# Windowed attention with an MLP mixer: where the loads, the casts and the global columns stand in the instruction order

## The chip, the cores and the metric

The kernel runs on one core of a Trainium2 chip. A core has five engines that each execute their own instructions in order and meet only at semaphores: TensorE (PE, with its weight loads listed as PEld), VectorE (DVE), ScalarE (ACT), GpSimd (POOL) and SyncE (SP). SP computes nothing here: it issues transfers and DMA transposes. POOL issues transfers too. All transfers are carried out by 16 DMA engines. SBUF is the working memory of 128 partitions, PSUM the memory that TensorE writes.

The metric is the device time of one execution in microseconds (us), less is better. A kernel's time is the median of its runs. One execution of each kernel was also taken with the profiler; times inside it count from the start of its span.

## The reference

A batch goes through attention with a window of 32 positions to each side and 8 global positions, and then through an MLP mixer over tokens and channels. Shapes: 8 batches, 8 heads, 576 positions, 64 values for each head; the mixer works on 576 x 512.

```python
def _attn_ref(q, k, v, global_idx):
    scores = scale * np.matmul(q, k.transpose(0, 1, 3, 2))
    mask = np.abs(pos[:, None] - pos[None, :]) <= window
    mask = mask | is_global[:, None] | is_global[None, :]
    scores = np.where(mask, scores, -1000000000.0)
    ...
    return np.matmul(attn, v)

def _moe_ref(x, w_tok1, w_tok2, w_ch1, w_ch2):
    xt = x.transpose(0, 2, 1)
    h = np.maximum(xt @ w_tok1, 0.0) @ w_tok2
    u = x + h.transpose(0, 2, 1)
    h2 = np.maximum(u @ w_ch1, 0.0) @ w_ch2
    return u + h2
```

## The kernel before

**Data.** Heads are taken in four pairs, positions in five tiles, the last of 64. Each batch needs q and k with positions along the free axis. They are loaded as f32 into `lq`, `lk` (1024 KB each) and `lr` (the last 64 positions, twice 128 KB), cast to f16 into `qk` and `rn`, turned, and put in order into `qT` and `kT`. `lq`, `lk`, `lr`, `qk` and `rn` exist once: a load waits until the casts of the batch before have read its buffer, a cast until the turns of the batch before have read its own. `qT` and `kT` exist twice. `qT` also holds eight global columns for each tile, copied by `globals_` (L377) from `gT`, which `gather_t` (L305) makes from the gathered rows of four batches: t=0 for batches 1 to 3, t=1 for batches 4 to 7.

**Two ways to turn.** Batches 0 to 2 are turned on TensorE: `T` (L401) transposes into PSUM, `TE` (L409) copies out of it on DVE with a shuffle, two copies for q and two for k. Batches 3 to 7 are turned by DMA transposes from SP (`turns`, L674), into `raw` and `rawr`, and put in order by DVE copies (`order`, L367).

**Attention of a batch n.** `S_all` (L468) multiplies q and k of one pair into two PSUM tiles of a pool of three (`psS`), and ACT takes their exps in three parts into `e_all`. `SM` (L471) multiplies by the band's mask on DVE. `GK` (L481) makes the rows of the global positions, `gk`, for which all four pairs of `qT` must be ready. `OG` and `PV` make the output x.

**Mixer.** `M1` and `M2` mix tokens and give `u`; `M3` (L607) transposes `u` by DMA from SP into `uT`, two tiles at a time and, after odd batches, the last rows `ul` of two batches. `M4` (L619) gives `b1` with a relu on ACT, `M5` (L644) multiplies by the second weight in two parts for each tile. The second part ends with a DVE add into `osb` and a store from SP. `osb` comes from a pool of three buffers (`ob`, L53), which a store gives back when it has landed. `M4` and `M5` use a PSUM pool of two (`psM`). After an odd batch there are five tiles t0 to t4, the last with the rest of two batches (add at L658, two stores at L660), otherwise four.

**Order.** The order of all instructions is written out by hand and each engine gets its own in that order. `period(b)` (L684) runs the attention of batch n = b + 1 and fills in the channel mixer of batch b: the list `dense` holds its M4 and M5 pieces, and `d(k)` puts in the next k of them. At a period's end some pieces are left over, which the next period begins with. m = b + 2 is the batch whose q and k are prepared meanwhile. In a period the emission is: scores of pairs 0, 1 and 2; GK; from the period of batch 3 on, the turns of m and the load of m + 1; scores of pair 3; OG; five PV with M1 between; M2 and M3; left-over pieces; and, last, `globals_(m)`.

**Loads and casts before.** The load of batch 1 is issued during batch 0; load(2) and load(3) stand at the heads of the periods of batches 1 and 2, load(4) behind the turns of batch 3, load(5) to load(7) behind the turns of 4 to 6. All loads are issued from SP. Batch 2 is cast in one block on ACT at the end of the period of batch 1, batch 3 on POOL during the period of batch 2. Batches 4 to 7 have nine casts each on ACT: three at a period's end, three behind the scores of pair 0 of the next period, three behind those of pair 1. The first of the nine is for `rn`, then q and k of one pair after the other.

Of the kernel before, what the change touches and what calls it, by code (L numbers as in the profile page):

```python
# [18 lines left out]
WIN = 32  # L19
# [7 lines left out]
def kernel(  # L27
# [12 lines left out]
    nc = tc.nc  # L40
    B, H, S, D = q.shape
# [7 lines left out]
    LAST = S - P * (NT - 1)  # L49
# [33 lines left out]
        r1 = P - WIN if c == NT - 1 else P  # L83
        return r0, r1, P * c - WIN + r0

    def load_qk(b, hs):
        for ten, dst in ((q, lq), (k, lk)):
            nc.sync.dma_start(
                out=dst[:, hs].rearrange("p h i d -> p h (i d)"),
                in_=ten[b, hs, 0 : S - LAST, :].rearrange("h (p i) d -> p h (i d)", i=4),  # L90
            )

    def load_rest(b):
        for t, ten in enumerate((q, k)):
            nc.sync.dma_start(
                out=lr[LAST * t : LAST * t + LAST], in_=ten[b, :, S - LAST : S, :].rearrange("h p d -> p h d")
            )

# [238 lines left out]
    def casts(b, eng):  # L337
        return [lambda: cast_qk(b, 0, None, eng)] + [
            lambda ti=ti, p=p: cast_qk(b, ti, p, eng) for p in range(NP) for ti in range(2)
        ]  # L340
# [68 lines left out]
    def TE(b, p):  # L409
        pT = st[b]["pT", p]  # L410
        qT, kT = qTs[b % 2][:, p], kTs[b % 2][:, p]

        pm = pT[:, 0, 0:512].rearrange("p (i t x) -> p t x i", i=4, t=4)
        nc.vector.tensor_copy(out=qT[:, 0:4, GW:QS].rearrange("p t (x i) -> p t x i", i=4), in_=pm)
        nc.vector.tensor_copy(out=qT[:, 4, GW : GW + LAST], in_=pT[:, 1, 512 : 512 + LAST])
        nc.vector.tensor_copy(  # L416
            out=kT[:, WIN : WIN + 512].rearrange("p (x i) -> p x i", i=4),
            in_=pT[:, 1, 0:512].rearrange("p (i x) -> p x i", i=4),
        )
        nc.vector.tensor_copy(out=kT[:, WIN + 512 : WIN + S], in_=pT[:, 1, 512 + LAST : 640])  # L420

    def S_(b, p, part):
        qf = qTs[b % 2][:, p].rearrange("p t x -> p (t x)")
# [44 lines left out]
    def S_all(b, p):  # L468
        return S_(b, p, 0) + S_(b, p, 1)
# [74 lines left out]
    def M1(b, ch):  # L544
        s = st[b]
        if ch == 0 and b == 0:
            s["a1p"] = [psm([P, 512], name=f"a1p_{b}_{tt}") for tt in range(2)]
        elif ch == 0:
            ps = pss([P, 2, 512], name=f"a1p_{b}")
            s["a1p"], s["a1pp"] = [ps[:, 0], ps[:, 1]], ps  # L550
        ps = s["a1p"]
        for tt in range(2):
            w = w1[:, ch, P * tt : P * tt + P] if ch < NT - 1 else w1l[:, b % 2, P * tt : P * tt + P]
            nc.tensor.matmul(ps[tt], lhsT=w, rhs=x16s[b % 2][:, ch, :], start=(ch == 0), stop=(ch == NT - 1))  # L554
        if ch < NT - 1:
            return
        a1 = mb.tile([P, 2, DM], F16, tag="a1", bufs=1, name=f"a1_{b}")
        if b == 0:
            nc.scalar.activation(out=a1[:, 0], in_=ps[0], func=AF.Relu)
            nc.vector.tensor_scalar(out=a1[:, 1], in0=ps[1], scalar1=0.0, scalar2=None, op0=ALU.max)  # L560
        else:
            nc.scalar.activation(out=a1, in_=s["a1pp"], func=AF.Relu)
        s["a1"] = a1
        s["u16"] = mb.tile([P, 4, DM], F16, tag="u16", name=f"u16_{b}")
        if b % 2 == 0:
            s["ul"] = mb.tile([P, DM], F16, tag="ul", name=f"ul_{b}")
        else:
            s["ul"] = st[b - 1]["ul"]
# [95 lines left out]
    def d(k):  # L664
        for _ in range(k):
            if dense:
                dense.pop(0)()

    def load(i):
        if i < B:  # L670
            load_rest(i)
            load_qk(i, slice(0, H))

    def turns(i):  # L674
        turn_rest(i)
        for p in range(NP):
            turn(i, p)

    def cast(i, lo, hi):
        if 3 < i < B:  # L680
            for c in casts(i, nc.scalar.copy)[lo:hi]:
                c()

    def period(b):  # L684
        n, m = b + 1, b + 2
        odd = b % 2
        dense.extend(lambda j=j: M4(b, j) for j in range(NJ))
        if odd:
            dense.extend(lambda j=j: M4l(b, j) for j in range(3))
        dense.extend(lambda t=t, i=i: M5(b, t, i) for t in range(4 + odd) for i in range(2))  # L690
        if n == B:
            d(len(dense))
            return
        tail = len(dense) - (23 if odd else 20) - 2 * odd
        regular = n > 2

        def scores(p):
            es = S_all(n, p)
            es[0]()
            es[1]()  # L700
            d(1)
            es[2]()
            if n < 3 and p < 2:
                T(n, p + 2)
            d(1)
            SM(n, p)
            if n < 3 and p < 2:
                TE(n, p + 2)
            elif n > 2 and p < 2:
                order(n, p + 2)  # L710

        if n == 1:
            load(2)
        elif n == 2:
            load(3)
        scores(0)
        cast(m, 3, 6)
        d(1 if tail > 5 else 0)
        scores(1)
        cast(m, 6, 9)  # L720
        d(max(tail - 4 - (tail > 5), 0))
        scores(2)
        GK(n)
        if regular and m < B:
            turns(m)
            load(m + 1)
        if n == 2:
            for c in casts(3, nc.gpsimd.tensor_copy):
                c()
            turns(3)  # L730
            load(4)
        d(1)
        scores(3)
        d(1)
        OG(n)
        d(1)
        if n == 3:
            gather_t(1)
        fill = [order_rest, lambda i: order_k(i, 0), lambda i: order_q(i, 0), lambda i: order_k(i, 1), lambda i: order_q(i, 1)]
        for tau in range(NT):  # L740
            PV(n, tau)
            if 0 < tau < 4:
                M1(n, tau - 1)
            if regular and m < B:
                fill[tau](m)
            if tau < 4:
                d(1)
        M1(n, 3)
        d(len(dense) - (8 + 2 * odd))
        M1(n, 4)  # L750
        d(1)
        if m < B:
            load_v16(m)
        M2(n, 0)
        M3(n, 0)
        M2(n, 1)
        M3(n, 1)
        M2(n, 2)
        if n % 2:
            M3(n, 2)  # L760
        if n == 1:
            for c in casts(2, nc.scalar.copy):
                c()
            d(2)
            T(2, 0)
            TE(2, 0)
            T(2, 1)
            TE(2, 1)
        else:
            cast(n + 2, 0, 3)  # L770
            d(1)
            if n == 2:
                order_rest(3)
                order(3, 0)
                order(3, 1)
            d(1)
        if m < B:
            globals_(m)

    def cast0(p):  # L780
        cast_qk(0, 0, p, nc.scalar.copy)
# [58 lines left out]
        M1(0, tau - 2)  # L840
    M1(0, NT - 2)
    M1(0, NT - 1)
    M23_first(0)
    M23_first(1)
    M3_first(0)
# [7 lines left out]
    T(1, 1)  # L853
    TE(1, 0)
    TE(1, 1)
    gather_t(0)
    globals_(1)
    qk_pads(1)
    pads(1)
    load_wc2(0)  # L860
# [36 lines left out]
```

## Time and profile before

| | |
|---|---|
| runs | 347.68, 350.14 and 350.29 us |
| median of the runs | 350.14 us |
| profiled execution | 347.81 us, of which its span 346.1 us |
| mean granted clock of TensorE | 0.982 |
| DVE, ACT, POOL busy | 58%, 48%, 21% of the span |
| moved by DMA | 48.18 MB, mean 139 GB/s |

The profiled execution is close to the fastest run. In the profile a line such as `x <- y` names the tile written and the tile read, `L651` the line of the kernel, and the bracket behind a row of the timeline gives how long the engine stood idle before it and what ended that idle time. SPq is SP's queue of issues: the time of such a row is that of the issue, not of the transfer. Times to landing stand in the view of the DMA issues. The granted clock is a share of TensorE's full speed.

### The profile page before, as it was taken

Reading aid. Unit: us, or ns where it says so; the run is one execution under the profiler, and the core shown is the slowest. Engines: PE = TensorE matmul, PEld = TensorE weight load, DVE = VectorE, ACT = ScalarE, POOL = GpSimd, SP = SyncE. Lnnn points to the kernel's source line nnn. Section 1 sums busy time; section 2 is a strip of 40 time slices with the busy share of each in tenths; the row PEclk is TensorE's granted clock in tenths of the full one; section 3 lists DMA queues with packets and bytes.
Section 4 is the critical chain, followed back from the end, with each engine's and each line's share of the span. In section 5 each row is a group of like instructions: output and inputs, shape, how many; then the busy total and the mean of one; then the engine's idle time right before and its main releaser. Section 6 shows DMA issues by size and latency. Waiting matters only on the chain.

```text
span 346.1 us, 6451 instructions
## 1 busy us (share of the span) xinstructions
PE 302.6 (87%) x2541; PEld 157.8 (46%) x2541; DVE 200.6 (58%) x433; ACT 165.3 (48%) x292; POOL 72.3 (21%) x113
## 2 busy tenths in 40 slices
PE   1556859997989979999899999997899999998994
PEld 0334435553436634464346544643356445543641
DVE  5898767648396456675757456763763666351021
ACT  2438137605482346732973577335945247303600
POOL 8879535100069100040004000310000000000000
PEclk9999989999899989999999999999999999999998
DMA  5999999603889992599549964999350421033013
GB/s 156 255 294 155 225 247 196 39 32 91 239 186 127 228 229 76 108 127 296 150 112 134 290 128 102 112 226 238 93 93 17 110 77 30 0 76 123 0 63 91
DMA packets 114526, 48.18 MB, mean 139 GB/s; under 512 B 89408, under 2 KB 109760, under 8 KB 114496
## 3 DMA queue, kind: packets, MB, share of 16 engines
q1 hardware_dynamic: 77008, 39.60, 49.3%
q0 software_dynamic: 37200, 8.16, 29.1%
q8 instruction: 20, 0.33, 0.4%
q14 instruction: 10, 0.08, 0.1%
q10 hardware_dynamic: 288, 0.01, 0.0%
HBM read 36.12 MB, written 9.44 MB: 132 GB/s over the span
## 4 chain that ended last, share of the span: by engine, by line
PE 62%; DVE 16%; DMA 9%; ACT 7%; SPq 3%; issue 2%; ACTq 0%; DVEq 0%
PE op L651 21%; PE b1p L625 18%; DMA lk<-in_k_dram 8%; PE a1p L554 4%; PE s L431 3%; PE b1lp L638 3%; DVE e_all L479 3%; PE hp L578 3%; ACT e_all L444 3%; PE pv L531 2%; PE pv L522 2%; PE pv L527 2%; DVE kT L416 2%; ACT b L628 1%; ACT e_all L457 1%
## 5 line engine op out<-in xcount | busy, mean ns | idle before, releaser
L625 PE MATMUL b1p<-uT,wc 128*128 128x512 f16 x384 | 96.1, 383 | 5.4 <-DVE osb L655 4.3
L651 PE MATMUL op<-wc,b 128*128 128x512 f16 x384 | 90.8, 389 | 0.0
L628 ACT ACTIVATE b<-b1p 128x512 f16<-128x512 f32 x96 | 58.5, 609 | 64.9 <-PE b1p L625 64.6
L651 PEld LDWEIGHTS <-b 128*128 128x128 f16 x384 | 37.2, 99 | 45.8 <-issue 3.4
L625 PEld LDWEIGHTS <-wc 128*128 128x128 f16 x384 | 34.9, 98 | 48.5 <-issue 10.9
L655 DVE TENSOR_TENSOR osb<-u,op 128x512 f32<-128x512 f16 x32 | 21.9, 685 | 53.5 <-PE op L651 50.2
L324 POOL DMA_DIRECT2D vsh<-in_v_dram x35 | 29.9, 865 | 103.9 <-PE pv L531 101.1
L444 ACT ACTIVATE e_all<-s 128x832 f16<-128x832 f32 x32 | 27.8, 869 | 39.4 <-issue 20.6
L479 DVE TENSOR_TENSOR e_all<-e_all,bandm 128x1040 f16<-128x1040 f16 x64 | 43.7, 723 | 1.2
L584 DVE TENSOR_TENSOR u<-x,hp 128x512 f16<-128x512 f16 x28 | 17.4, 682 | 22.1 <-PE hp L578 22.1
L431 PE MATMUL s<-qT,kT 64*128 64x208 f16 (+1 forms) x320 | 20.9, 257 | 10.4 <-DVE qT L378 6.3
L539 DVE TENSOR_TENSOR x<-pv,rr 128x512 f16<-128x512 f32 (+1 forms) x40 | 27.6, 691 | 1.4
L522 PEld LDWEIGHTS <-e_all 128*128 128x128 f16 x320 | 22.1, 100 | 5.5 <-issue 0.5
L473 DVE TENSOR_TENSOR eg<-e_all,bandm 128x160 f16<-128x160 f16 x32 | 7.8, 245 | 28.8 <-ACT e_all L462 28.6
L522 PE MATMUL pv<-vsh,e_all 128*128 128x66 f16 x320 | 24.4, 197 | 0.0
L431 PEld LDWEIGHTS <-kT 64*128 64x128 f16 x320 | 12.5, 98 | 25.2 <-issue 16.1
L335 ACT CAST qk<-lq 128x512 f16<-128x512 f32 x28 | 17.8, 634 | 12.3 <-DMA lq<-in_q_dram 12.2
L457 ACT ACTIVATE e_all<-s 128x576 f16<-128x576 f32 x32 | 21.0, 657 | 3.2 <-PE s L431 3.2
L538 DVE RECIPROCAL rr<-pv 128x8 f32<-128x8 f32 (+1 forms) x40 | 8.3, 207 | 23.1 <-PE pv L531 22.9
L527 PE MATMUL pv<-vsh,e_all 128*128 128x66 f16 x256 | 21.1, 198 | 0.0
L335 ACT CAST qk<-lk 128x512 f16<-128x512 f32 x24 | 15.3, 638 | 11.6 <-DMA lk<-in_k_dram 11.6
L527 PEld LDWEIGHTS <-e_all 128*128 128x128 f16 x256 | 17.9, 101 | 3.5 <-issue 0.2
(154 smaller groups left out, 348.4 us busy)
## 6 DMA issues: line engine op xcount, KB each, us to landing
out_dram<-osb SPq DMA_DIRECT2D x32, 256.0 KB, 2.3
lq<-in_q_dram SPq DMA_DIRECT2D x7, 1024.0 KB, 7.4
lk<-in_k_dram SPq DMA_DIRECT2D x7, 1024.0 KB, 10.3
wc<-in_moe_w_ch_dram POOLq DMA_DIRECT2D x6, 512.0 KB, 12.9
vsh<-in_v_dram POOLq DMA_DIRECT2D x21, 128.0 KB, 5.8
vsh<-in_v_dram POOLq DMA_DIRECT2D x14, 96.0 KB, 6.2
lq<-in_q_dram SPq DMA_DIRECT2D x4, 256.0 KB, 5.3
lk<-in_k_dram SPq DMA_DIRECT2D x4, 256.0 KB, 5.7
```

What stands on the lines that cost most here:

```text
L324: nc.gpsimd.dma_start(out=vsh[b % 2][r0:r1, c, :, 0:D], in_=v[b, :, j0 : j0 + (r1 - r0), :].rearrange("h p d -> p h d"),)
L335: eng(out=qk[:, ti, p].rearrange("q i (r d) -> q r i d", r=2), in_=(lq, lk)[ti][:, hs])
L431: nc.tensor.matmul(ps[:, par, off : off + n], lhsT=kT[r, P * c : P * c + P], rhs=qf[r, lo : lo + n], start=True, stop=True,)
L444: nc.scalar.activation(out=e2[:, :, 1:3, 64:EW], in_=ps[:, :, 0 : 2 * W].rearrange("p h (c x) -> p h c x", c=2), func=AF.Exp, scale=scale,)
L457: nc.scalar.activation(out=o, in_=ps[:, :, 0 : 2 * QS].rearrange("p h (c x) -> p h c x", c=2), func=AF.Exp, scale=scale)
L479: nc.vector.tensor_mul(out=eh, in0=eh, in1=bandm)
L522: nc.tensor.matmul(o, lhsT=e_all[:, h, tau, EW - P - sh : EW - sh], rhs=vsh[b % 2][:, tau, h, :], start=hh == 0, stop=False,)
L527: nc.tensor.matmul(o, lhsT=e_all[:, h, tau + 1, 0:P], rhs=vsh[b % 2][:, tau + 1, h, :], start=False, stop=False)
L539: nc.vector.tensor_tensor(out=x16s[b % 2][r, tau, :].rearrange("p (f h x) -> p f h x", f=2, h=NP), in0=pq[r, :, :, 0:D], in1=rr[r].unsquee ...
L625: nc.tensor.matmul(ps, lhsT=wc1[:, cc, P * j : P * j + P], rhs=s["uT"][:, cc, :], start=(cc == 0), stop=(cc == 3))
L628: nc.scalar.activation(out=s["b1"][:, j, :], in_=ps, func=AF.Relu)
L651: nc.tensor.matmul(ps, lhsT=w, rhs=wc2[:, j, :], start=(j == 0), stop=(j == NJ - 1))
```

## The change

- Loads: at the head of a period of batch n >= 3 the kernel issues load(n + 2), ahead of the scores and of everything that the period issues from SP. Before, that load stood behind the turns of n + 1 in the same period. Load(2) goes out through POOL; load(3) and load(4) stay where they were.
- Casts: the nine casts of a batch from 4 on stand in one block on ACT at the end of the period before, behind M3 and ahead of the left-over pieces.
- Left-over pieces: the pieces that stood behind the scores of pairs 0 and 1 (with the casts) now stand within them, ahead of `SM` and `order`. No product on TensorE changes its place by this.
- Global columns: `globals_(m)` stands ahead of the last but one M1 instead of at the period's end; `gather_t(0)` and `globals_(1)` stand ahead of `M23_first`, instead of behind the shuffles of batch 1.
- The k copies of `TE` for pairs 0 and 1 of batch 1 go from DVE to ACT.

```diff
-    def load_qk(b, hs):
+    def load_qk(b, hs, eng=None):
         for ten, dst in ((q, lq), (k, lk)):
-            nc.sync.dma_start(
+            (eng or nc.sync).dma_start(
...
+        copy_k = nc.scalar.copy if b == 1 and p < 2 else nc.vector.tensor_copy
...
-        nc.vector.tensor_copy(
+        copy_k(
             out=kT[:, WIN : WIN + 512].rearrange("p (x i) -> p x i", i=4),
...
-        nc.vector.tensor_copy(out=kT[:, WIN + 512 : WIN + S], in_=pT[:, 1, 512 + LAST : 640])
+        copy_k(out=kT[:, WIN + 512 : WIN + S], in_=pT[:, 1, 512 + LAST : 640])
...
     def load(i):
+        eng = nc.gpsimd if i == 2 else nc.sync
         if i < B:
-            load_rest(i)
-            load_qk(i, slice(0, H))
+            load_rest(i, eng)
+            load_qk(i, slice(0, H), eng)
...
-        def scores(p):
+        def scores(p, k):
...
-            d(1)
+            d(1 + k)
             SM(n, p)
...
-        if n == 1:
-            load(2)
-        elif n == 2:
-            load(3)
-        scores(0)
-        cast(m, 3, 6)
-        d(1 if tail > 5 else 0)
-        scores(1)
-        cast(m, 6, 9)
-        d(max(tail - 4 - (tail > 5), 0))
-        scores(2)
+        load(2 if n == 1 else 3 if n == 2 else n + 2)
+        scores(0, tail > 5)
+        scores(1, max(tail - 4 - (tail > 5), 0))
+        scores(2, 0)
         GK(n)
         if regular and m < B:
             turns(m)
-            load(m + 1)
...
+        if m < B:
+            globals_(m)
         M1(n, 3)
...
+        later = 2 if n == 1 else n + 2
+        if later < B:
+            for c in casts(later, nc.scalar.copy):
+                c()
         if n == 1:
-            for c in casts(2, nc.scalar.copy):
-                c()
             d(2)
...
         else:
-            cast(n + 2, 0, 3)
             d(1)
...
-        if m < B:
-            globals_(m)
...
     M1(0, NT - 1)
+    gather_t(0)
+    globals_(1)
     M23_first(0)
...
-    gather_t(0)
-    globals_(1)
     qk_pads(1)
```

More of the change, by code (lines that the diff above doesn't have):

```diff
@@ L91, in load_qk, with load_rest @@
             )
-    def load_rest(b):
+    def load_rest(b, eng=None):
         for t, ten in enumerate((q, k)):
-            nc.sync.dma_start(
+            (eng or nc.sync).dma_start(
                 out=lr[LAST * t : LAST * t + LAST], in_=ten[b, :, S - LAST : S, :].rearrange("h p d -> p h d")
@@ L677, in turns @@
             turn(i, p)
-    def cast(i, lo, hi):
-        if 3 < i < B:
-            for c in casts(i, nc.scalar.copy)[lo:hi]:
-                c()
     def period(b):
@@ L732, in period @@
         d(1)
-        scores(3)
+        scores(3, 0)
         d(1)
@@ L760, in period @@
             M3(n, 2)
+        later = 2 if n == 1 else n + 2
+        if later < B:
+            for c in casts(later, nc.scalar.copy):
+                c()
         if n == 1:
-            for c in casts(2, nc.scalar.copy):
-                c()
             d(2)
```

## The prediction

> **What bounds the kernel now.** I read the page's head first, then PE's idle gaps in the timeline, the granted clock around them, and last what fills SP's queue. A head is the start of a period, where the scores of the next batch begin; heads are numbered by that batch, 1 to 7.
>
> ```profile
> span 346.1 us, 6451 instructions
> PE 302.6 (87%) x2541; PEld 157.8 (46%) x2541; DVE 200.6 (58%) x433; ACT 165.3 (48%) x292; POOL 72.3 (21%) x113
> ```
>
> TensorE is busy for 87% of the span and executes in order, so a piece of another engine counts only where it makes PE wait. These places are the heads: the scores need shuffled q and k, global columns, exps on ACT and free buffers at once. The view by windows shows two of them (columns: stretch, its length, PE, PEld, DVE, ACT and POOL busy, granted clock, DMA share, GB/s).
>
> ```profile
> 45.90:50.05 4.15, 0.39 (x4) 0.20 (x4) 3.72 (x14) 0.00 (x0) 1.03 (x1) 1.00 1.34 275
> 50.05:53.50 3.45, 3.45 (x23) 2.03 (x24) 0.00 (x0) 2.00 (x4) 1.72 (x2) 0.51 2.22 174
> 84.40:87.00 2.60, 0.02 (x2) 0.02 (x4) 2.52 (x9) 0.00 (x0) 0.00 (x0) 1.00 0.51 99
> 87.60:91.00 3.40, 3.40 (x16) 1.82 (x15) 0.00 (x0) 1.64 (x3) 0.00 (x0) 0.50 0.74 171
> ```
>
> PE does nothing for 3.8 and 2.6 us while DVE is busy, and then runs some 3.4 us at half clock. Such a gap costs its length and 1.7 us (half of 3.4) behind it.
>
> **First head: gathered rows and two copies.** The rows are DVE, DVE, then PE.
>
> ```profile
> 45.17 0.68 DVE L587 TENSOR_TENSOR ul<-x,hp 64x512 f16<-64x512 f16 x1 [1.10 <-PE hp L578]
> ...
> 48.56 0.20 DVE L308 CAST g_q<-g_q 128x128 f16<-128x128 f32 x1
> ```
> ```profile
> 50.05 0.94 PE L431 MATMUL s<-qT,kT 64*128 64x208 f16 x10 [0.87 <-DVE qT L378]
> ```
> ```profile
> 85.34 0.68 DVE L414 COPY qT<-pT 128x512 f16<-128x512 f16 x1
> ...
> 86.73 0.19 DVE L378 COPY qT<-gT 128x160 f16<-128x160 f16 x1
> ```
>
> Today `ul` (45.17) is followed by both pairs' shuffles, then by gathered rows and global columns from 48.56, and the scores start at 50.05, 1.49 us later. The change puts that block ahead of M23_first, where PE and DVE wait for each other anyway. There it costs between nothing and its 1.49 us; I take 0.8, the middle. After `ul` (0.68) only the first pair's q copies are left, one copy of 0.68 (row at 85.34) and a short one: the next group of four copies starts 1.39 us (86.73 - 85.34) after this pair's begin, so q is half, 0.7. The k copies go to ACT beside it. Scores start at about 45.2 + 0.8 + 0.7 + 0.7 = 47.4, 2.65 us sooner, and the half clock (1.7) should go, since PE's gap shrinks below 1 us. That is 4.35; I take 4.1, because the next shuffles still follow the exps on DVE.
>
> Load(2) moves to POOL. It is issued behind gather(1) and its data is first read by the casts at the end of the period (before the gap at 84.40), so I cost it at nothing. POOL has room for four issues:
>
> ```profile
> POOL rn L332 <- PE pT L406: 32.3, 1, 32.3
> ```
>
> Were the cover gone, the casts and with them head 2 would be late by the overhang.
>
> **Second head: global columns earlier.** Scores wait for the global columns (86.73, 0.19) behind the second pair's shuffles; afterwards only for the first pair, done at 85.34. The gap loses 1.6 us (86.92 - 85.34), is then 1.0, and the half clock behind it (1.7) goes. PE would be about 4.1 + 1.6 + 1.7 = 7.4 us ahead.
>
> **Third head: the loads do not come along.** Load(3) is followed by casts on POOL, transposes on SP, load(4) on SP and casts(4) on ACT. This chain gains only the 4.1 of the first head. Casts(4) now stand in one block of nine ahead of the exps. The rows: ACT, then the row of PE that ends this head's scores, the global rows' products `gk`.
>
> ```profile
> 126.40 0.62 ACT L335 CAST qk<-lk 128x512 f16<-128x512 f32 x1 [3.63 <-DMA lk<-in_k_dram]
> ...
> 128.60 0.63 ACT L335 CAST qk<-lq 128x512 f16<-128x512 f32 x1
> 129.11 0.64 ACT L335 CAST qk<-lk 128x512 f16<-128x512 f32 x1
> ```
> ```profile
> 138.75 0.36 PE L488 MATMUL gk<-qT,kgz 128*32 128x384 f16 x4
> ```
>
> The first k cast, held by its load, starts at 126.40 - 4.1 = 122.3. Seven casts at 0.51 (129.11 - 128.60) end near 125.9, and only then come the exps, one cast later than k's arrival before, seven casts now. So the 7.4 us of PE shrink to about 1 here. Load(5) stands on SP at this head, and its k half waits for the last k cast: issued about 126.1.
>
> In heads 4 to 6 the load is early and the cast block is hidden, as ACT's rows of head 5 show:
>
> ```profile
> 193.09 1.02 ACT L562 ACTIVATE a<-a1p 128x1024 f16<-128x1024 f32 x1
> ...
> 199.50 0.86 ACT L444 ACTIVATE e_all<-s 128x832 f16<-128x832 f32 x1 [0.27 <-PE s L431]
> ```
>
> From 194.1 nine casts take 4.7 us and end at 198.8, ahead of the exp at 199.5. Without that cover a block would cost up to 3.1 (six casts).
>
> **What is behind the load on SP.** A load is followed by stores of `osb`. The trace has one such store: rows of SP (issues), then of DMA issues (KB, us to landing), the usual landing of a store, and the one wait for a store.
>
> ```profile
> 87.45 0.62 SPq L95 DMA_DIRECT2D lr<-in_q_dram  x1
> ...
> 89.53 1.04 SPq L88 DMA_DIRECT2D lk<-in_k_dram  x1
> 93.17 0.36 SPq L656 DMA_DIRECT2D out_dram<-osb  x1
> ```
> ```profile
> lk<-in_k_dram SPq DMA_DIRECT2D x1, 1024.0 KB, 9.2
> out_dram<-osb SPq DMA_DIRECT2D x1, 256.0 KB, 6.2
> ```
> ```profile
> out_dram<-osb SPq DMA_DIRECT2D x32, 256.0 KB, 2.3
> ```
> ```profile
> DVE osb L655 <- DMA out_dram<-osb: 3.1, 1, 3.1
> ```
>
> That store took 6.2 us instead of 2.3 and landed at 99.4, 0.6 after lk (98.7): it went through behind the load. From the first issue of a load to the landing of a store behind it pass 11.9 us (99.4 - 87.45). `osb` has three buffers, and DVE has waited for a store once. Heads 3, 5 and 7 have seven M5 pieces left over, which fill four `osb` (t1 to t4); heads 4 and 6 have five pieces and three `osb`, one of which takes t0's buffer, stored ahead of the load. So in heads 3 and 5, with a load in front, t4 must wait until t1's store has landed. Head 7 has no load.
>
> The Trainium skill (DMA: Bandwidth & Descriptors, section "Queues, rings and completion order") says that completion is not in order per issuing engine. If that freed the store, t4 would not wait; the row above shows none of this freedom.
>
> The M5 pieces also move ahead of SM on DVE. Then t4's `osb`, SM of pair 1 and its order stand in a row before `gk`. Rows of head 5, DVE and PE, and SP's u transposes:
>
> ```profile
> 206.85 0.69 DVE L655 TENSOR_TENSOR osb<-u,op 128x512 f32<-128x512 f16 x1 [1.98 <-PE op L651]
> 207.45 0.23 DVE L473 TENSOR_TENSOR eg<-e_all,bandm 128x160 f16<-128x160 f16 x1
> ...
> 208.95 0.59 DVE L356 COPY kT<-raw 128x512 f16<-128x512 f16 x1
> ...
> 209.97 0.68 DVE L658 TENSOR_TENSOR osb<-ul,op 128x512 f32<-128x512 f16 x1
> ```
> ```profile
> 203.55 0.57 PE L431 MATMUL s<-qT,kT 64*128 64x208 f16 x10
> ...
> 209.33 0.57 PE L431 MATMUL s<-qT,kT 64*128 64x208 f16 x10
> ...
> 211.66 0.36 PE L488 MATMUL gk<-qT,kgz 128*32 128x384 f16 x4
> ```
> ```profile
> 195.94 6.25 SPq L614 DMA_TRANSPOSE uT<-u  x4
> ```
>
> DVE takes 0.60 + 1.50 + 1.02 = 3.1 us (206.85 to 209.97) from an `osb` to the end of the order; with two hand-overs of 0.1, `gk` follows the last M5 piece by 3.3. Today PE needs 2.33 between (209.33 to 211.66). Every head from 4 on pays 1.0 for this, even where no store is late.
>
> **Sum, head by head, at `gk`.**
> Head 3: lk(5) issued 126.1, landed +9.2, store +0.6: 136.0 (rounded up); +3.1 and 0.1 for the hand-over: 139.2, before 138.75. Loss 0.4; all that was gained is spent. Were the store not late: scores of pair 1 after the first exp at about 126.7 (125.9 and 0.86), 5.8 us of pieces (203.55 to 209.33), +3.3: 135.8, a gain of 2.9.
>
> Head 4, with the load early and the casts done, loses its waits:
>
> ```profile
> 165.84 0.39 PE L431 MATMUL s<-qT,kT 64*128 64x144 f16 x6 [0.36 <-ACT e_all L444]
> ...
> 170.16 0.57 PE L431 MATMUL s<-qT,kT 64*128 64x208 f16 x10
> ...
> 174.22 0.36 PE L488 MATMUL gk<-qT,kgz 128*32 128x384 f16 x4
> ```
> ```profile
> 239.39 0.39 PE L431 MATMUL s<-qT,kT 64*128 64x144 f16 x6 [1.77 <-ACT e_all L444]
> ...
> 243.71 0.57 PE L431 MATMUL s<-qT,kT 64*128 64x208 f16 x10
> ...
> 247.77 0.36 PE L488 MATMUL gk<-qT,kgz 128*32 128x384 f16 x4
> ```
>
> Pieces end at 170.16 - 0.36 - 0.2 (the head's own wait for global columns, as long as that copy's 0.19) = 169.6; `gk` 172.9; gain 1.3. Head 6 likewise: 243.71 - 1.77 - 0.2 = 241.7, `gk` 245.0, gain 2.8.
>
> Head 5: the u transposes start at 195.94; without a load before them they should take less than today's 6.25, so with t0's store the load starts about 201.7. Store of t1 lands at 201.7 + 11.9 = 213.6, `gk` at 213.6 + 3.2 = 216.8 instead of 211.66: loss 5.1. PE's gaps there are about 3 us before the second M4 piece and 1.7 before `gk`. I add 1.2 for the half clock (1.7 in seven of ten cases). Loss 6.3; ends 3.5 (a load 2 us faster, no half clock) and 8.5.
>
> The Trainium skill (TensorE: Matmul & The Clock Gate, section "Why this matters for your kernels") allows gaps up to about 3 us before the clock drops. By it the 1.2 would be left out; the row of 2.60 us here was followed by half clock all the same.
>
> Head 7: loss 1.0.
>
> Sum: +0.4 - 1.3 + 6.3 - 2.8 + 1.0 = +3.6. The profiled execution took 347.8 (span 346.1), so 351.4 on its scale. The median of the three runs is 350.1, 2.3 above it (one run at 347.7, two at 350.1 and 350.3); on that scale 353.7. I say 353.
>
> **Rivals.**
> Stores are not held (faster): they land among the load, or `osb` has a buffer to spare. Head 3 then gains 2.9, head 5 loses only 1.0: -2.9 - 1.3 + 1.0 - 2.8 + 1.0 = -5.0, or 345 beside the median; if load(4) came early enough as well, head 3 would keep all 7.4 instead of 2.9, hence 340.5. For it: the gaps at heads 1 and 2 are real, and the wait for a store is there only once. Against it: the store at 93.17. Chance 0.30.
>
> Longer third and fifth heads (slower still): PE stands over 4 us at head 3 while the cast block ends, and the transposes of the next batch, queued behind the load too, come late for the orders among the PV pieces. Head 3 loses 3, head 5 8.5: 350.1 + 3 - 1.3 + 8.5 - 2.8 + 1 = 358.5. For it: the half clock after gaps; against it: the u transposes, of which head 3 has need first, now go ahead of the load. Chance 0.13.
>
> It cancels: head 3 gains 1 to 2 and the store in head 5 lands 2 us sooner: 350 to 351. Chance 0.10.
>
> **How the numbers follow.** My forecast has 0.47. It centres on +3.6 us, just where 1% begins (3.5; about what a measurement of this kernel can tell from no change), so I count 0.30 of it slower and 0.17 the same. Faster: 0.30 from the first rival. Same: 0.17 + 0.10 = 0.27. Slower: 0.30 + 0.13 = 0.43. The range from 342 to 358 takes in the first rival's 345 with 3 us below it, the forecast with both its ends, and the slower rival almost to its centre; left out are the early load(4) and the worst. The forecast's own range is 350 to 356.
>
> **What would show it.** Right: DVE's wait for `out_dram` grows from 3.1 to some 8 us, on the `osb` of the left-over row block (L658's) at heads 3 and 5; ACT's casts no longer wait for loads at heads 4 and 6, but still at head 3; no half clock in the first 90 us; PE waits for the order copies before `gk`. Wrong: stores behind a load that land in 2 to 3 us; head 3's k cast far before 122; a gain of heads 1 and 2 that is still there at PV of batch 3.

## The result, and the profile after

The changed kernel takes 352.8 us (median of 5 runs, 351.39 to 354.11), the kernel before 350.08 (median of 5, 347.68 to 350.29). The ratio of the means (352.97 and 349.37) is 1.0103, with a 95% interval of 1.0056 to 1.015: about 1% slower, and no change (1.0) lies outside the interval. The forecast was 353.0.

The profiled execution of the changed kernel took 353.93 us. The head of its page:

```profile
span 352.2 us, 6450 instructions
...
PE 304.0 (86%) x2541; PEld 157.3 (45%) x2541; DVE 197.7 (56%) x429; ACT 167.3 (47%) x296; POOL 74.9 (21%) x117
```

The span grew by 6.1 us, the medians by 2.7, the means by 3.6. The profiled execution before was 2.3 below its kernel's median (347.81 against 350.08), the one after is 1.1 above; together that is the difference between 6.1 and 2.7. So the profiles overstate the loss, and steps are compared here within them. 0.9 us of it stands ahead of everything that the change touches: TensorE's last row before the block of gathered rows starts at 39.32 before and at 40.19 after. In the twelve profiles here that row starts anywhere from 38.87 to 40.34 us. In the table this 0.9 is part of head 1.

The table gives the start of the last row of `gk` products of each head in the timeline, in us from the span's start, and what each head adds.

| head | before | after | after - before | step of this head | forecast's step |
|---|---|---|---|---|---|
| 1 | 59.96 | 57.52 | -2.44 | -2.4 | -4.1 |
| 2 | 98.49 | 92.65 | -5.84 | -3.4 | -3.3 |
| 3 | 138.92 | 141.62 | +2.70 | +8.5 | +7.8 |
| 4 | 174.39 | 175.50 | +1.11 | -1.6 | -1.3 |
| 5 | 211.84 | 218.93 | +7.09 | +6.0 | +6.3 |
| 6 | 247.95 | 253.19 | +5.24 | -1.9 | -2.8 |
| 7 | 285.39 | 291.57 | +6.18 | +0.9 | +1.0 |

All signs are as forecast. The change loses 14.5 us in heads 3 and 5 and 0.9 in head 7, and wins 9.3 in heads 1, 2, 4 and 6.

**Heads 1 and 2.** PE's rows that wait there, in the timeline of the changed kernel (start, length, what ran, and in brackets the idle time before it and what ended it):

```profile
49.02 0.57 PE L432 MATMUL s<-qT,kT 64*128 64x208 f16 x10 [1.30 <-ACT kT L417]
```
```profile
82.81 0.57 PE L432 MATMUL s<-qT,kT 64*128 64x208 f16 x10 [1.07 <-DVE kT L417]
```

Gaps of 2.9 and 2.7 us have become 1.3 and 1.1, and no half clock is left in the first 120 us. At head 1 the scores wait for the k copy that went to ACT.

**Head 3.** ACT, then SP's issues, then PE:

```profile
125.06 0.62 ACT L335 CAST qk<-lk 128x512 f16<-128x512 f32 x1 [2.85 <-DMA lk<-in_k_dram]
...
128.19 0.61 ACT L335 CAST qk<-lk 128x512 f16<-128x512 f32 x1
128.71 0.85 ACT L445 ACTIVATE e_all<-s 128x832 f16<-128x832 f32 x1
```
```profile
126.15 0.65 SPq L95 DMA_DIRECT2D lr<-in_q_dram  x1
...
128.83 0.49 SPq L88 DMA_DIRECT2D lk<-in_k_dram  x1
129.41 2.73 SPq L657 DMA_DIRECT2D out_dram<-osb  x2
```
```profile
129.61 0.60 PE L432 MATMUL s<-qT,kT 64*128 64x144 f16 x6 [6.97 <-ACT e_all L445]
...
141.46 0.32 PE L489 MATMUL gk<-qT,kgz 128*32 128x384 f16 x1 [1.08 <-DVE qT L362]
```

Seven casts run one behind the other from the arrival of k, and the first exp only then. PE stands for 6.97 us. Load(5) is issued around the last casts, its k half right behind the last of them, and two stores stand behind it.

**Head 5.** Issues on SP, how long the stores took (the view of DMA issues from 200 to 217 us: KB, median us to landing), DVE and PE:

```profile
203.78 0.64 SPq L95 DMA_DIRECT2D lr<-in_q_dram  x1
...
206.48 3.20 SPq L657 DMA_DIRECT2D out_dram<-osb  x3
```
```profile
out_dram<-osb SPq DMA_DIRECT2D x4, 256.0 KB, 7.9
```
```profile
215.40 0.69 DVE L659 TENSOR_TENSOR osb<-ul,op 128x512 f32<-128x512 f16 x1 [6.83 <-DMA out_dram<-osb]
```
```profile
216.14 1.87 PE L626 MATMUL b1p<-uT,wc 128*128 128x512 f16 x4 [4.24 <-DVE osb L659]
```

Here the load was in time and no cast was late, and yet PE stood for 4.24 us: `osb` had no free buffer, because the store that held it had gone out behind the load. (The x4 take in t0's store, ahead of the load, which landed in 2.2; the three behind it took 7.9 to 8.8.) The list of waits counts both places:

```profile
DVE osb L659 <- DMA out_dram<-osb: 9.8, 2, 6.8
...
PE b1p L626 <- DVE osb L659: 4.6, 2, 4.2
...
PE gk L489 <- DVE qT L362: 2.8, 4, 1.1
```

The clock's share of it stands in the view by windows (stretch, length, PE, PEld, DVE, ACT, POOL busy, granted clock, DMA share, GB/s):

```profile
211.89:215.30 3.41, 0.01 (x1) 0.00 (x0) 0.00 (x0) 1.22 (x3) 0.00 (x0) 1.00 1.02 357
215.30:218.71 3.41, 2.57 (x11) 0.59 (x11) 3.28 (x7) 0.60 (x1) 0.00 (x0) 0.50 0.47 113
218.72:222.13 3.41, 3.41 (x17) 1.16 (x17) 1.84 (x4) 1.69 (x4) 0.00 (x0) 0.50 0.55 111
```

After the gap PE works 2.57 + 3.41 = 6.0 us at half clock, which costs 3.0.

### The profile page after: what moved, and what is told of

Read it like the earlier page. It is cut to its first block, busy times and chain, and to the rows that moved or that the text cites. A ratio compares the mean times of both kernels' runs of the same rounds, so it can differ in the third digit from the quotient of the medians.

```text
span 352.2 us, 6450 instructions
## 1 busy us (share of the span) xinstructions
PE 304.0 (86%) x2541; PEld 157.3 (45%) x2541; DVE 197.7 (56%) x429; ACT 167.3 (47%) x296; POOL 74.9 (21%) x117
## 4 chain that ended last, share of the span: by engine, by line
PE 57%; DVE 15%; DMA 15%; ACT 5%; SPq 4%; issue 3%; POOL 1%; DVEq 0%; ACTq 0%; POOLq 0%
PE op L652 20%; PE b1p L626 15%; DMA lk<-in_k_dram 8%; DMA out_dram<-osb 6%; PE a1p L555 4%; PE hp L579 4%; DVE e_all L480 4%; PE pv L523 2%; PE pv L532 2%; PE s L432 2%; PE b1lp L639 2%; PE pv L528 2%; SPq L349 2%; ACT e_all L445 1%; DVE osb L656 1%
## 5 line engine op out<-in xcount | busy, mean ns | idle before, releaser
L652 PE MATMUL op<-wc,b 128*128 128x512 f16 x384 | 89.5, 384 | 0.0
L585 DVE TENSOR_TENSOR u<-x,hp 128x512 f16<-128x512 f16 x28 | 17.4, 682 | 21.4 <-PE hp L579 21.4
L335 ACT CAST qk<-lq 128x512 f16<-128x512 f32 x28 | 17.5, 625 | 4.8 <-DMA lq<-in_q_dram 4.8
L555 PE MATMUL a1p<-x,w 128*128 128x512 f16 x64 | 19.3, 387 | 0.0
```

Of the source, the lines that this page charges most:

```text
L652: nc.tensor.matmul(ps, lhsT=w, rhs=wc2[:, j, :], start=(j == 0), stop=(j == NJ - 1))
```

## The experiments

The runs of the kernel before that stood beside them had medians of 349.53, 348.69 and 349.31 us. "Ratio" is that of the means to the kernel before, with its 95% interval; the changed kernel's is 1.0103. Differences to the changed kernel are those of the medians; by the ratios they come out up to 0.8 us otherwise.

**1. More buffers for osb.** The theory: the stores behind the load, and nothing else, make head 5 late.

```diff
-    ob = ctx.enter_context(tc.tile_pool(name="ob", bufs=3))
+    ob = ctx.enter_context(tc.tile_pool(name="ob", bufs=5))
```

> The changed kernel with five osb buffers instead of three. Theory (stores queued behind the load keep osb buffers busy): DVE's wait of L659 for out_dram, 9.8 us in two waits, goes to zero; at head 5 PE's 4.24 us gap before the second M4 piece and the half clock behind it go, gk there comes 5 to 6 us sooner; head 3 gains about 1, because its 7 us gap before the scores of pair 1 comes from the casts and stays. About 347 (344 to 348.5). Rival (SM and order behind the add into osb are what costs, the stores are harmless): within 1 us of 352.8.

Measured: 345.82 us, ratio 0.9903 (0.9868 to 0.9938). DVE's row of head 5 now waits for PE, and PE's gap of head 3 is unchanged:

```profile
209.65 0.69 DVE L659 TENSOR_TENSOR osb<-ul,op 128x512 f32<-128x512 f16 x1 [1.90 <-PE op L652]
```
```profile
129.76 0.59 PE L432 MATMUL s<-qT,kT 64*128 64x144 f16 x6 [7.12 <-ACT e_all L445]
```

The stores still land late (7.5 to 8.9 us for the three behind the load of head 5), but nobody waits for them; the change is now a gain. From head 4 to head 5 the kernel takes 38.39 us at `gk` (174.68 to 213.07) against 37.45 before and 43.43 in the changed kernel, so the late store was 5.0 of head 5's 6.0, and the order of the pieces the other 0.9. Head 3 gains only 0.8: with the casts late, the wait for a buffer there was hardly on PE's path. The prediction had put 3.4 on it.

**2. The first two heads alone.** The kernel before, with only the gathered rows, the global columns, the k copies on ACT and load(2) on POOL.

```diff
+    gather_t(0)
+    globals_(1)
     M23_first(0)
...
+        copy_k = nc.scalar.copy if b == 1 and p < 2 else nc.vector.tensor_copy
...
+        eng = nc.gpsimd if i == 2 else nc.sync
...
+        if m < B:
+            globals_(m)
         M1(n, 3)
```

> The kernel before with the edits of the first two heads alone: gather_t(0), globals, the k copies on ACT, load(2) through POOL; loads 5 to 7, casts and left-over pieces as before. Theory (head 3 is pinned to the chain of loads 3 and 4): gk of head 2 about 5.8 us sooner, the first k cast of batch 4 only 1 to 2 us sooner, so most of it is lost in a gap of PE at head 3: 346 to 349. Rival (the gain of the first heads carries through): 344.5 or less.

Measured: 345.94 us, ratio 0.9894 (0.986 to 0.9928), at the lower edge of the theory's range. At `gk` it is 6.4 us ahead of the kernel before at head 2, and 1.5 at head 3, because k of batch 4 arrives only 1.45 us sooner (cast 124.95 against 126.40) and PE waits for it:

```profile
124.95 0.62 ACT L335 CAST qk<-lk 128x512 f16<-128x512 f32 x1 [3.65 <-DMA lk<-in_k_dram]
```
```profile
126.38 0.59 PE L432 MATMUL s<-qT,kT 64*128 64x144 f16 x6 [4.59 <-ACT e_all L445]
```

**3. SM and order ahead of the left-over pieces.** The changed kernel, with the left-over pieces behind `SM` and `order`, as they were.

```diff
-            d(1 + k)
+            d(1)
             SM(n, p)
...
+            d(k)
```

> The changed kernel with the left-over pieces behind SM and order again, as before the change; three osb buffers. Theory (the add into osb ahead of SM and order holds up gk): the wait of gk for DVE's order, 0.6 us at heads 4, 6 and 7 and 1.1 at head 3, goes; at heads 3 and 5 SM no longer stands behind the add that waits for a store, so gk follows the second M4 piece at once, 1 to 2 us sooner. 348 to 350.5, while L659 still waits for out_dram. Rival (the order on DVE is without effect, since PE waits for the PSUM buffer of t4 anyway): 352 to 353.

Measured: 349.52 us (median of 10), ratio 1.0019 (0.9995 to 1.0043), 3.3 below the changed kernel. PE's waits for the order copies are gone. The wait for the store at head 5 shrinks, but PE still stands for it:

```profile
214.79 0.69 DVE L659 TENSOR_TENSOR osb<-ul,op 128x512 f32<-128x512 f16 x1 [4.04 <-DMA out_dram<-osb]
```
```profile
215.53 1.82 PE L626 MATMUL b1p<-uT,wc 128*128 128x512 f16 x4 [3.97 <-DVE osb L659]
```

From one `gk` to the next, heads 4 to 7 take 1.0 to 1.5 us less each than in the changed kernel. So the place of the pieces is a price of its own, beside the stores.

**4. Loads, casts and pieces alone.** The changed kernel with the first-head edits undone. I held that what they gain is spent by head 3, as the prediction says.

```diff
-    gather_t(0)
-    globals_(1)
     M23_first(0)
...
-        copy_k = nc.scalar.copy if b == 1 and p < 2 else nc.vector.tensor_copy
...
-        eng = nc.gpsimd if i == 2 else nc.sync
+        eng = nc.sync
...
-        if m < B:
-            globals_(m)
         M1(n, 3)
```

> The changed kernel with the edits of the first two heads undone: loads, cast block and left-over pieces alone. Theory (what the first heads gain is spent at head 3): only the 1.4 us by which the chain of loads starts later, 353.5 to 356, with no 7 us gap at head 3. Rival (the first heads' 5.8 us are in the changed kernel's time): 358.5.

Measured: 359.12 us, ratio 1.0275 (1.0235 to 1.0315). My theory was wrong, the rival right. Three rows show why (SP, POOL, ACT):

```profile
87.65 0.63 SPq L95 DMA_DIRECT2D lr<-in_q_dram  x1
...
112.29 0.62 SPq L95 DMA_DIRECT2D lr<-in_q_dram  x1
```
```profile
100.81 0.68 POOL L335 CAST qk<-lk 128x512 f16<-128x512 f32 x1 [2.61 <-DMA lk<-in_k_dram]
```
```profile
129.32 0.62 ACT L335 CAST qk<-lk 128x512 f16<-128x512 f32 x1 [2.27 <-DMA lk<-in_k_dram]
```

The same rows of the changed kernel stand at 84.89, 107.69, 96.72 and 125.06. The 2.8 us by which load(3) is issued later have become 4.3 at the first k cast of batch 4, and `gk` of head 3 is 4.1 later (145.70 against 141.62). Beside the changed loads the first heads' edits are worth some 6 us of median, not the 1 to 3 that I had left to them. Against the kernel before, though, load(3) was issued at the same time (87.45) and load(4) 2.7 later. SP's rows show where: the issue of the last rows of k took 1.97 us instead of 0.65, so that the turns began 1.55 later, and the turns took 14.01 instead of 12.86. Nothing found in the edit explains the longer issue, and its cause stays open.

**5. The stores on POOL's queue.** The changed kernel, three buffers, both `out` stores issued by POOL. The question: does the order on SP's queue hold the stores, or the traffic of the load?

```diff
-                nc.sync.dma_start(out=out[b, P * tau : P * tau + P, :], in_=osb)
+                nc.gpsimd.dma_start(out=out[b, P * tau : P * tau + P, :], in_=osb)
```

> The changed kernel with the stores of osb issued through POOL, three buffers as before. Theory (order within SP's queue holds the stores): they land in 3 to 5 us although the load runs beside them, L659 waits under 1 us, 346 to 349. Rival (the load takes the DMA engines themselves, whichever queue the store is in): stores beside the load still take over 7 us, L659 still waits some 5 us, 351 or more.

Measured: 344.59 us, ratio 0.9855 (0.9807 to 0.9903), below what the theory had. DVE's `osb` of head 5 waits for no store, while a load of the same size runs. Below it are two of POOL's issues, and the large stores issued from 196 to 200 us and from 201.7 to 206:

```profile
206.54 0.69 DVE L659 TENSOR_TENSOR osb<-ul,op 128x512 f32<-128x512 f16 x1 [1.90 <-PE op L652]
```
```profile
199.15 0.56 POOL L657 DMA_DIRECT2D out_dram<-osb  x1 [2.22 <-DVE osb L656]
201.74 0.54 POOL L657 DMA_DIRECT2D out_dram<-osb  x1 [2.03 <-DVE eg L474]
```
```profile
out_dram<-osb POOLq DMA_DIRECT2D x2, 256.0 KB, 2.7
```
```profile
out_dram<-osb POOLq DMA_DIRECT2D x2, 256.0 KB, 6.8
```

The load's first issue stands at 199.10. The stores of t0 and t1 went out before it and beside it and landed in 2.7 us; those of t2 and t3, issued into its traffic, took 7.5 and 6.1, not much less than the 7.9 to 8.8 on SP's queue. So the theory's 3 to 5 us beside a load is not borne out, and the load's traffic is most of what makes a store slow. What freed the buffer is that t1's store was issued 1.0 us after its add began (198.16); it landed at 201.83, long before t4's add at 206.54. On SP it was issued 4.4 after the add (202.09 and 206.48), behind the u transposes, t0's store and the load's issues. Something is left to the queue: the two slow stores landed at 209.24 and 210.99, ahead of the load's k half (212.10), and in the changed kernel no store behind a load did that. Unasked for, k of batch 4 came sooner too (cast at 122.18), to which runs 9 and 10 return.

**6. Head 3.** The changed kernel; the nine casts of batch 4 again in three parts, and load(5) through POOL behind the scores of pair 2.

```diff
-        eng = nc.gpsimd if i == 2 else nc.sync
+        eng = nc.gpsimd if i in (2, 5) else nc.sync
...
-        load(2 if n == 1 else 3 if n == 2 else n + 2)
+        if n != 3:
+            load(2 if n == 1 else 3 if n == 2 else n + 2)
         scores(0, tail > 5)
+        if n == 3:
+            for c in casts(4, nc.scalar.copy)[3:6]:
+                c()
         scores(1, max(tail - 4 - (tail > 5), 0))
+        if n == 3:
+            for c in casts(4, nc.scalar.copy)[6:9]:
+                c()
         scores(2, 0)
+        if n == 3:
+            load(5)
...
-            for c in casts(later, nc.scalar.copy):
+            for c in casts(later, nc.scalar.copy)[: 3 if n == 2 else 9]:
```

> The changed kernel with head 3 as before: casts of batch 4 in three parts, load(5) behind the scores of pair 2 and through POOL. Theory (at head 3 the cast block and the load in front of the stores cost): first exp 3.1 us nearer to the first k cast, PE's gap before the scores of pair 1 falls from 7 to about 4 us, no wait for a store there; gk of head 3 about 4 us sooner; heads 4 to 7 unchanged: 348 to 349.5. Rival (gk of head 3 hangs on the chain of loads alone): 352 or more.

Measured: 345.27 us, ratio 0.9901 (0.9878 to 0.9924), better than the theory had it. ACT and PE of head 3:

```profile
122.31 0.62 ACT L335 CAST qk<-lk 128x512 f16<-128x512 f32 x1 [2.36 <-DMA lk<-in_k_dram]
```
```profile
123.74 0.39 PE L432 MATMUL s<-qT,kT 64*128 64x144 f16 x6 [1.08 <-ACT e_all L445]
```

The gap falls from 6.97 to 1.08 us; head 5 keeps its own of 4.07. Two things shortened it, of which I had counted one: the exp stands behind one cast instead of seven, and k came 2.75 us sooner.

**7. All three repairs.** Five buffers (run 1), pieces behind `SM` (run 3), and head 3 as in run 6; the edits beside run 6's:

```diff
-    ob = ctx.enter_context(tc.tile_pool(name="ob", bufs=3))
+    ob = ctx.enter_context(tc.tile_pool(name="ob", bufs=5))
...
-            d(1 + k)
+            d(1)
             SM(n, p)
...
+            d(k)
```

> The changed kernel with five osb buffers, left-over pieces behind SM, and head 3 as in the run before this one. If the three costs add, about 6.5 + 2.5 + 3 us come off 352.8, since the wait for the store at head 3 counts once: 339.5 to 343. Rival (they overlap, as SM behind the late add is part of the store's cost): 343 to 345.5.

Measured: **335.28 us** (333.99 to 335.65), ratio 0.9625 (0.9607 to 0.9642). It beats both kernels, the changed one by 17.5 us, and is 4 us below what its parts gave me. Runs 1, 3 and 6 measured the three parts at 7.0, 3.3 and 7.5 us, 17.8 together: within the scatter of the runs they add.

```profile
span 332.2 us, 6435 instructions
...
PE 297.7 (90%) x2541; PEld 156.0 (47%) x2541; DVE 198.0 (60%) x429; ACT 166.0 (50%) x296; POOL 79.4 (24%) x121
```

Behind head 1 PE never stands longer than 1.15 us in one gap up to head 7, and the clock is full until the last microsecond.

**8. The same, stores on POOL.** As run 7, with three buffers and the stores through POOL, to see whether another queue beats more buffers.

```diff
-    ob = ctx.enter_context(tc.tile_pool(name="ob", bufs=5))
+    ob = ctx.enter_context(tc.tile_pool(name="ob", bufs=3))
...
-                nc.sync.dma_start(out=out[b, P * tau : P * tau + P, :], in_=osb)
+                nc.gpsimd.dma_start(out=out[b, P * tau : P * tau + P, :], in_=osb)
```

> The same with the stores through POOL and three osb buffers, instead of five buffers. Theory (SP's queue is what holds the stores, and without them SP's transposes and loads of batches 3 and 4 come sooner): first k cast of batch 4 about 3 us sooner than with the stores on SP, so 1 to 2 us below the run before this one: 338 to 342. Rival (POOL, waiting for each add, is late with v and load(5)): above 343.

Measured: 341.22 us (339.06 to 344.07), ratio 0.9817 (0.9746 to 0.9887). It does not. The time lies in the theory's range, but k of batch 4 is cast at 123.01, not sooner than in run 7 (121.53). PE has gaps there that run 7 lacks (1.64 us for `uT` at 89.4, 1.57 for x at 181.7); they make up half of the 5.9 us. Some 1.5 more fall behind head 7: from its `gk` to the end the runs with five buffers (1, 7 and 9) take 59.2 to 59.5 us, run 8 60.9. Where the rest lies is not shown.

**9. v loads beside load(4).** In runs 5 to 8 the time from load(4)'s first issue to the first k cast was 12.5 to 12.8 us, in the two kernels and runs 1 to 4 16.8 to 18.3. Common to the four was that POOL issues the v loads of batch 4 later, behind something that waits. Run 9 is run 7 with only these five v loads put back ahead of load(5).

```diff
         if n == 3:
+            load_v16(4)
             load(5)
...
-        if m < B:
+        if m < B and n != 3:
             load_v16(m)
```

> The kernel of e7_all, with the five v loads of batch 4 ahead of load(5) on POOL instead of behind it, so that they are issued at about 107 us, beside load(4), as in the changed kernel. Theory (v loads beside load(4) slow it): the time from load(4)'s first issue to the first k cast goes from 12.6 back to about 17 us, the first k cast starts at about 125 to 126 instead of 121.5, head 3 ends 3 to 4 us later and the kernel takes 338 to 340 us. Rival (the v loads do not matter; load(4) came sooner for another reason, as fewer stores or POOL's own place): the k cast stays within 1 us of 121.5 and the time within 1.5 us of e7_all's 335.3.

Measured: 339.47 us, ratio 0.9742 (0.971 to 0.9775), 4.2 above run 7; the intervals lie apart. POOL and ACT of run 9, then of run 7:

```profile
101.30 8.36 POOL L324 DMA_DIRECT2D vsh<-in_v_dram  x10
```
```profile
126.69 0.62 ACT L335 CAST qk<-lk 128x512 f16<-128x512 f32 x1 [5.64 <-DMA lk<-in_k_dram]
```
```profile
102.59 4.19 POOL L324 DMA_DIRECT2D vsh<-in_v_dram  x5
```
```profile
121.53 0.62 ACT L335 CAST qk<-lk 128x512 f16<-128x512 f32 x1 [2.29 <-DMA lk<-in_k_dram]
```

Ten v loads in a row instead of five, and k is cast 5.2 us later, though its load was issued 1.7 sooner (107.20 against 108.91). The view of the DMA issues gives lk(4) 17.0 us to landing in run 9, 10.5 in run 7 and 15.0 in the changed kernel. PE stands 6.31 us at head 3 again. So where the v loads stand is the cause.

**10. load(5) on POOL alone.** The changed kernel with only load(5) moved, casts in one block.

```diff
-        eng = nc.gpsimd if i == 2 else nc.sync
+        eng = nc.gpsimd if i in (2, 5) else nc.sync
...
-        load(2 if n == 1 else 3 if n == 2 else n + 2)
+        if n != 3:
+            load(2 if n == 1 else 3 if n == 2 else n + 2)
...
         scores(2, 0)
+        if n == 3:
+            load(5)
```

> The changed kernel with load(5) alone moved: through POOL, behind the scores of pair 2; the casts of batch 4 stay in one block, osb keeps three buffers, the pieces stay ahead of SM. Theory (load(5) on POOL holds the v loads of batch 4 back, so load(4) lands sooner, and the store of head 3 is no longer behind a load): first k cast at about 122.5 instead of 125.06, PE's gap of 6.97 us at head 3 shrinks to about 4 to 4.5, no wait of head 3 for out_dram, head 5 as before; 3 to 5 us below the changed kernel: 348 to 350 us. Rival (the split of the casts is what made e6_head3 fast): k cast stays near 125, the gap near 7, and only the wait for the store goes: 351 to 353 us.

Measured: 347.24 us (median of 9), ratio 0.9945 (0.9923 to 0.9968), 5.6 below the changed kernel, somewhat more than expected. k is cast at 119.94, the gap of head 3 is down to 4.22, and only head 5 still waits for a store:

```profile
124.49 0.52 PE L432 MATMUL s<-qT,kT 64*128 64x144 f16 x6 [4.22 <-ACT e_all L445]
```

So of the 7.5 us of run 6 over the changed kernel, 5.6 come from this one load's queue and place, and some 2 from splitting the casts (1.5 by the ratios, whose intervals just touch): the block was the smaller part of head 3.

## Why the prediction was right, and where it was not

**The store behind the load: right in cause, and in size at head 5 alone.** From a load's first issue to the landing of a store behind it the prediction took 11.9 us. Head 3 shows 12.1 from that issue to the end of DVE's wait (126.15 to 138.22), head 5 11.6 (203.78 to 215.40). The wait came on the left-over row block's `osb`, at heads 3 and 5, 9.8 us together where some 8 were named. Runs 1 and 5 remove it in two ways, and both become faster than the kernel before: 345.8 and 344.6, where the first rival's price was 345. That rival was wrong of this kernel. That its price fits run 1 is luck in part: at `gk` of head 3 it had a gain of 2.9, and run 1 is 1.9 behind the kernel before there (140.80 against 138.92). The price of the late store at head 3 was mis-sized: the prediction put 3.4 on it (139.2 against 135.8 without it), and run 1 gives 0.8, because the way without it is late as well. In run 1 the first k cast starts at 125.21, 2.9 later than forecast, and behind PE's gap of 7.12 the clock is halved for two stretches of 3.41 us, in which PE works 4.0 us: 2.0 lost, for which head 3 had no term. 135.8 with both is 140.7, and the last pair's `gk` starts there at 140.64. The Trainium skill (DMA: Bandwidth & Descriptors, section "Queues, rings and completion order") says that completion is not in order per issuing engine. It promises no order; but on SP's queue no store got past the load in front of it: at heads 3, 4 and 5 the first one behind it landed 0.7 us after the load's k half.

**Head 5: 6.0 instead of 6.3, from other parts.** Of the 6.0 at `gk`, PE's gap is 4.24 and longer work 1.74, of which 1.4 is half clock (2.79 us of PE's work at half, up to `gk`). The prediction had 5.1 and 1.2. But the half clock goes on behind `gk` for another 3.2 us, 1.6 us lost, which the table books on head 6. Without it head 6 gains about 3.5, more than the 2.8 forecast. The clock term was too small: 3.0 in all instead of 1.2, because it lasted two stretches of 3.41 us and not one.

**Order behind the pieces: right in size.** PE's wait before `gk` is only 0.57 to 0.58 us at heads 4, 6 and 7, but the price is the 1.0 of the prediction: head 7 is 0.9 longer, run 1 puts it at 0.9 between heads 4 and 5, and undoing it in run 3 takes 1.0 off heads 4, 5 and 7 and 1.5 off head 6, 3.3 of the time in all.

**Head 1: 2.4 instead of 4.1.** Half of the 1.7 is not the change's: the profile of the changed kernel is 0.87 late at the last row ahead of the block (PE, before, then after). Behind it, the changed kernel's `ul` and its first k copy (DVE, then ACT):

```profile
39.32 0.59 PE L554 MATMUL a1p<-x,w1l 128*128 128x512 f16 x2
```
```profile
40.19 0.59 PE L555 MATMUL a1p<-x,w1l 128*128 128x512 f16 x2
```
```profile
46.97 0.68 DVE L588 TENSOR_TENSOR ul<-x,hp 64x512 f16<-64x512 f16 x1 [1.10 <-PE hp L579]
```
```profile
48.38 0.59 ACT L417 COPY kT<-pT 128x512 f16<-128x512 f16 x1 [1.37 <-DVE qT L416]
```

`ul` starts 1.80 us later than before (45.17); less 0.87, the block of gathered rows cost 0.9, where 0.8 was taken. The term that failed is the copies. The k copies were put "beside" DVE's, but ACT's k copy itself waited for DVE's q copy and ended last (gap of 1.30), so the scores began 2.05 behind `ul`, at 49.02, and not 1.4 behind it: 0.65 of the 1.7.

**Head 3: +2.7 instead of +0.4.** The step that failed is "the first k cast starts at 122.3". It started at 125.06, and from there everything ran as forecast: casts, load(5)'s k half at 128.8 instead of 126.1, `osb` at 138.2 instead of 136.0, `gk` 3.4 later. The cast was late because head 1 brought 2.4 and not 4.1 (0.9 of it the late start), of which load(4)'s issue kept 1.9 (107.69 against 109.59), and because the load then took 17.4 us to the cast instead of 16.8. "All that was gained is spent" was right for the profile, at 5.84 turned into a loss, but wrong as a statement about the edits: run 4 shows that without them head 3 is another 4.1 late.

**Heads 4 and 6** gained by the early load as said; ACT's casts wait for k once on a load in the whole kernel, at head 3 (2.85 us). **The sum** was 2.5 short in the profile (+3.6 against +6.1), 2.3 of it in by head 3, and 0.9 of that the late start. That the time came out within 0.2 us is luck in part. On the scale of the median the sum was 353.7, and 353 was said without a reason. I added the 2.3 by which the profiled execution before lay under its median, and then measured medians 2.7 apart (means 3.6), less than the profiles. Why the two profiled executions lie so to their medians is not settled.

**The second rival, longer third and fifth heads,** was half right. Head 3 came out at the 3 that it named, and for the reason it named, casts while PE stands. Head 5 was 6.0, not its 8.5.

## What to carry to other kernels

Here a load moved to the front of SP's queue delayed every store that was issued behind it until the whole load had landed; before moving a load, count the buffers that those stores give back, and add buffers or issue the stores elsewhere. A gain at one head passes on only through the chain that sets the next head, so follow the loads and not TensorE alone. Where transfers of another queue need not run yet, hold them back behind something that waits: five v loads beside a load cost 4 us here, more than splitting a block of casts gained.

## What the runs showed of the hardware

**The half clock goes by stretches of 3.41 us on a fixed grid.** The forecast took 1.7 us for any gap above some length. Ten of the twelve profiles here have half clock between heads 1 and 7. Its stretches begin and end on a grid of 3.41 us, the same within an execution, and PE's idle time within one stretch decides over the next. Before, at head 3, the stretch has 2.26 us of PE's idle in it, all of one gap:

```profile
121.75:125.16 3.41, 1.15 (x14) 0.56 (x12) 2.65 (x8) 0.62 (x1) 0.00 (x0) 1.00 1.37 260
125.16:128.57 3.41, 3.41 (x9) 1.18 (x8) 0.69 (x1) 2.17 (x4) 0.00 (x0) 0.50 1.49 138
```

In run 4 a longer gap of 2.59 us (131.28 to 133.87) is cut by the grid at 132.30 into 1.0 and 1.6, and the clock stays full:

```profile
128.88:132.30 3.42, 2.40 (x14) 0.98 (x13) 0.69 (x1) 2.98 (x6) 0.00 (x0) 1.00 1.09 203
132.30:135.71 3.41, 1.84 (x13) 0.87 (x13) 0.89 (x3) 3.41 (x7) 0.00 (x0) 1.00 0.84 200
135.71:139.12 3.41, 3.41 (x17) 1.57 (x16) 2.28 (x5) 0.75 (x2) 0.00 (x0) 1.00 1.05 353
```

From full clock, every stretch with 2.26 us or more idle was followed by half clock, and none with up to 1.64; no stretch of these profiles lies between. To come back takes more: a stretch at half clock with 0.65 to 3.4 us idle was followed by another at half (head 5 above, 0.84 idle in 215.30 to 218.71), one with up to 0.39 by full clock. So a gap of 4 us costs 1.7 us behind it (4.22 at head 3 of run 10, one stretch) or some 3 (4.24 at head 5 of the changed kernel, two), by where it falls, which is why the prediction's 1.2 became 3.0. The Trainium skill (TensorE: Matmul & The Clock Gate, section "Why this matters for your kernels") advises against idle gaps above about 3 us, since one window of idle halves the clock; here gaps of 2.26 to 2.7 us were enough when they fell into one stretch.

**What a v load costs a load beside it is more than its bytes.** Five v loads of 96 to 128 KB (0.6 MB) beside a load of 2.25 MB stretched the landing of its last megabyte from 10.5 to 17.0 us (runs 7 and 9), a factor of 1.6 for a quarter more bytes asked for. The v loads of batch 3, issued just ahead, ran in that time too. From load(4)'s first issue to the first k cast, POOL's queue shows this (number of packets, MB, share of 16 engines; run 7, then run 9):

```profile
q0 software_dynamic: 1393, 0.17, 21.8%
```
```profile
q0 software_dynamic: 7108, 1.14, 80.0%
```

These are some 125 and 160 bytes a packet, and 5700 packets more ran beside the load, at four times the share of the engines' time. That the number of packets and not the bytes sets the price fits this, but no run separates the two.
